# A state-space convolution and a gated linear unit on one core: three Fourier stages on sums and differences, split tokens kept in DRAM, and a new end of the program

## The chip, the core and the metric

The kernel runs on one of the eight cores of a Trainium2 chip. A core has a matrix engine (PE, with PEld for its weight loads), a vector engine (DVE), a scalar engine (ACT), GpSimd (POOL, used here to issue accumulating transfers), SyncE (SP, which issues the other transfers) and 16 DMA engines. Every engine works through its own instructions in order and waits on semaphores. The metric is device microseconds of one execution. Before the change three runs took 617.34, 618.17 and 620.17 us; the median is 618.17 us.

## The reference, cut to what matters

```
g = sigmoid((x * gate_w).sum(-1, keepdims=True))        # x is A_u, 2048 tokens x 512 channels
dt = exp(log_dt);  A = -exp(log_A_real) + 1j * A_imag;  C = (C_real + 1j * C_imag) * dt[:, None]
K = 2.0 * einsum("dn,dnl->dl", C, exp(A * dt * l)).real  # 512 channels, 128 states, l = 0..2047
a = irfft(rfft(x.T, 4096) * rfft(K, 4096))[:, :2048].T + x * D_skip
b = ((x @ w_gate) * (x @ w_up)) @ w_down                 # 512 -> 1792 -> 512, no nonlinearity
return g * a + (1 - g) * b
```

All of it is fp32. A convolution over 2048 tokens is done by Fourier transforms of length 4096, and a bilinear gated linear unit (GLU) over the same tokens is mixed with it.

## The kernel before, in words

**GLU.** The 1792 hidden features are 14 tiles of 128, taken in five groups (`GROUPS`: 3, 2, 3, 3, 3 tiles); inside a group the tokens pass in four sets of 512. Each fp32 operand is split into a high and a low fp32r part (`split`: a cast on ACT, a subtraction on DVE), and a product is three matmuls (low x high, high x low, high x high). `hidden(f)` makes 24 matmuls `pg` and `pu` of 128x512 for one tile of features, then ACT copies `pg` to `h`, DVE multiplies by `pu`, and ACT and DVE split the product into `hh` and `hl`. `down` multiplies by `w_down` into `y`: 12 matmuls per feature tile and set, so 36 per tile and set and 2016 in all. `evacuate` scales `y` by 1-g on ACT and sends it to the output, from the second group on as an accumulating transfer of POOL. `tokens` loads the four 128-channel pieces of a set and splits them, sixteen sets in all: four in the first group, three in each later one, since the order of the sets turns round from group to group.

**Convolution.** Channels go in 16 blocks of 32 for the kernel K and in 4 blocks of 128 for the transforms. For a block of 32, DVE and ACT make two tables of complex powers, `x` and `v` (`x_table`, `v_table`), and `k_block` multiplies them on PE (64 small matmuls, "kgen" below) into 2048 values of K, copied by ACT into `kt`. After each fourth block `k_first` takes the first Fourier stage of K. `u_part` does the same for the tokens, two columns of 128 rows at a time (eight parts), and DVE computes the gate's scores in it. Both stages write their spectra to DRAM (`su_d`, `sk_d`). `transforms(q)` then works on a block of 128 channels: `m_load` reads a quarter of both spectra, `m_second` is the second stage on PE, `m_product` the complex product on DVE, `m_inverse` the first inverse stage (through DRAM, `y_d`), `m_last` the last stage; its result is scaled by the gate and added to the output by POOL. "Second", "inverse" and "last" below are the PE tasks of these functions.

**Order.** Nothing is left to a scheduler: `Work` holds every piece as a task with an engine, a cost, a rank, what it reads and writes and the buffers that it holds. `Work.run` plans them on these costs and writes down each engine's order; `InOrder` binds the engines to it. `T_STEP` sets the earliest planned time of each GLU step. Every tile name has a fixed number of buffers, and a task that needs one waits for the last reader of the buffer's earlier content. A transfer that waits on SP holds up all that stand behind it on SP. The last rows of the output (set 3 of the last group) are finished in `ends`: they are read back into SBUF, added up there, and stored.

Of the kernel before, what the change touches and what calls it, by code (L numbers as in the profile page):

```python
# [10 lines left out]
F32 = mybir.dt.float32  # L11
# [3 lines left out]
ALU = mybir.AluOpType  # L15
# [27 lines left out]
N2 = list(range(1, 32, 2)) + list(range(2, 32, 4)) + list(range(0, 32, 8)) + list(range(4, 32, 8))  # L43
K_COLS = [[(0, 16, 16)], [(32, 8, 40), (48, 4, 52), (56, 4, 60)]]

def fourier_matrices():

    n1, k1 = np.arange(64), np.arange(64)
    ang = 2 * np.pi * np.outer(n1, k1) / 128
    c = np.stack([np.cos(ang), -np.sin(ang)], 2)
    c[:, 0, 1] = (-1.0) ** n1
    c = c.reshape(64, P)
    w1 = np.tile(c, (2, 1))
    w1k = np.tile(np.stack([c[2 * np.array(K_ROWS) + b] for b in range(2)], 1), (4, 1, 1))
    n2, k2 = np.array(N2), np.arange(32)
    w2 = np.zeros((2, 2, 32, 32, 2, 32))  # L60
    w3 = np.zeros((4, 32, 8, 2, 2, 2, 32))
    w4 = np.zeros((P, 64))
    s = 1 / 4096
    for k in range(64):
        S, j, e = k // 8, k // 2 % 4, k % 2
        q = k // 2
        if k:
            ph = 2 * np.pi * np.outer(n2, k + 128 * k2) / 4096
            co, si = np.cos(ph), np.sin(ph)
            w2[e, 0, :, q, 0], w2[e, 1, :, q, 0] = co, si  # L70
            w2[e, 0, :, q, 1], w2[e, 1, :, q, 1] = -si, co
            w3[j, :, S, e, 0, 0], w3[j, :, S, e, 0, 1] = 2 * s * co.T, 2 * s * si.T
            w3[j, :, S, e, 1, 0], w3[j, :, S, e, 1, 1] = -2 * s * si.T, 2 * s * co.T
            w4[2 * k], w4[2 * k + 1] = np.cos(ang[:, k]), -np.sin(ang[:, k])
            continue

        for l in range(1, 32):
            h, f = (0, 128 * l) if l < 16 else (1, 64 + 128 * (l - 16))
            ph = 2 * np.pi * n2 * f / 4096
            co, si = np.cos(ph), np.sin(ph)  # L80
            w2[0, h, :, 0, 0, l], w2[0, h, :, 0, 1, l] = co, -si
            w3[0, l, 0, 0, 0, h], w3[0, l, 0, 0, 1, h] = 2 * s * co, -2 * s * si
        w2[0, 0, :, 0, 0, 0], w2[0, 0, :, 0, 1, 0] = 1.0, (-1.0) ** n2
        w3[0, 0, 0, 0, 0, 0], w3[0, 0, 0, 0, 1, 0] = s, s * (-1.0) ** n2
        w4[0], w4[1] = 1.0, (-1.0) ** n1

    w4 = w4.reshape(2, 4, 2, 2, 4, 64).transpose(0, 2, 1, 3, 4, 5).reshape(P, 64)
    parts = (w1, w1k, w2.reshape(P, 32, 64), w3.reshape(P, 8, 2, 2, 64), w4)
    return [np.ascontiguousarray(a, np.float32) for a in parts]
# [24 lines left out]
T_STEP = 10.3  # L114
# [169 lines left out]
def gated_mix_kernel(  # L284
# [32 lines left out]
    m_su, m_sk, m_y, m_out = (work.memory() for _ in range(4))  # L317
# [12 lines left out]
    def inp(shape):  # L330
        return new("mid", "in", shape, bufs=3)
# [4 lines left out]
    half_pi = const.tile([P, 1], F32, name="half_pi")  # L336
    shift = const.tile([P, 1], F32, name="shift")
    gate = const.tile([P, NR], F32, name="gate")
    ngate = const.tile([P, NR], F32, name="ngate")
    score = const.tile([P, NR], F32, name="score")  # L340
# [4 lines left out]
    w1_t = tpool.tile([P, P], F32, name="w1_t")  # L345
    w1k_t = tpool.tile([P, 2, P], F32, name="w1k_t")
    skip = tpool.tile([P, 4, 32], F32, name="skip")
    m_const, m_powers, m_w1, m_w1k, m_skip = (work.memory() for _ in range(5))
# [3 lines left out]
    gw = new("mid", "bd", [P, D])  # L352
# [22 lines left out]
    def split(hi, lo, s, key):  # L375
# [5 lines left out]
        ph, pl = (hi, s), (lo, s)  # L381
        at = lambda x: x.t if s is None else x.t[:, s * D : (s + 1) * D]
        add("act", 0.62, lambda: act.copy(at(hi), src()), r=[got], w=[ph], rank=0)
        add(
            "dve", 0.69,
            lambda: dve.tensor_tensor(out=at(lo), in0=src(), in1=at(hi).bitcast(F32), op=ALU.subtract),
# [14 lines left out]
    def first_loads():  # L401
        in_y = lambda shape: new("mid", "y", shape, bufs=2)
        in_ev = lambda shape: new("mid", "ev", shape, bufs=3)
# [10 lines left out]
        for f in (1, 2):  # L414
            load_two(lambda k, f=f: ("w", f, k), in_ev, wts[f][:, : 2 * D].rearrange("p (k d) -> p k d", k=2))
# [51 lines left out]
    def product(pg, which, w, x, kt, after, first):  # L467
# [5 lines left out]
        def fn():  # L473
            for n, (a, b) in enumerate(three):
                pe.matmul(
                    pg.t, w[a].t[:, base : base + P], x[b].t, start=kt == 0 and n == 0, stop=kt == KT - 1 and n == 2
                )

        add("pe", 0.681, fn, r=[(w[0], part), (w[1], part), x[0], x[1]], w=[pg], rank=2, after=after)
# [43 lines left out]
    def evacuate(gi, ci, r, y):  # L523
        t = 4 * ci + r
        if gi == len(GROUPS) - 1 and ci == LAST:
            ending.append((r, y))
            return
        acc = new("glu", "acc", [P, D], bufs=3)
# [4 lines left out]

        if gi == 0:
# [7 lines left out]
    def ends():  # L542
# [7 lines left out]
        for r, y in ending:  # L550
            t = t0 + r
            add(
                "dve", 0.25,
                lambda r=r: dve.tensor_tensor(
                    out=sums.t[:, r, P * (KT - 1) :], in0=sums.t[:, r, P * (KT - 1) :], in1=late["fin"].t[:, r],
                    op=ALU.add,
                ),
                r=[late["fin"]], w=[(sums, r)], rank=0,
            )
            add(  # L560
                "dve", 0.69,
                lambda r=r, t=t, y=y: dve.scalar_tensor_tensor(
                    sums.t[:, r], y.t, ngate[:, t : t + 1], sums.t[:, r], op0=ALU.mult, op1=ALU.add
                ),
                r=[y, (m_gate, LAST)], w=[(sums, r)], rank=0,
            )
            add(
                "sp", 0.42, lambda r=r, t=t: sp.dma_start(ov[:, t, :], sums.t[:, r]), r=[(sums, r)], w=[(m_out, t)],
# [37 lines left out]
    def u_part(c):  # L606
        ut = inp([P, 2, D])
        add("sp", 0.42, lambda: sp.dma_start(ut.t, uv[:, 2 * c : 2 * c + 2, :]), w=[ut], dma=512, after=9.0 + 15.0 * c)

        def score_of(j):  # L610
            r = 2 * c + j
# [4 lines left out]
                    pr.t, ut.t[:, j, :], 1.0, gw.t, op0=ALU.mult, op1=ALU.mult, accum_out=score[:, r : r + 1]  # L616
                ),
                r=[ut, gw], w=[pr, (m_gate, ("s", c // 2))], rank=0,
            )


        banks = [[bank() for _ in range(2)] for _ in range(2)]
        sts = [stage([P, 2, D]) for _ in range(2)]

        def fn():
            for j in range(2):
                for h in range(2):
                    half = slice(64 * h, 64 * h + 64)
                    pe.matmul(
                        banks[j][h].t, w1_t[half], ut.t[half, j, :], start=True, stop=True, tile_position=(64 * h, 0)  # L630
                    )

        for j in range(2):
            score_of(j)
        add("pe", 2.08, fn, r=[ut, m_w1], w=banks[0] + banks[1], rank=1, hold=sts)
# [687 lines left out]
```

## Time and profile before

| | |
|---|---|
| median of three runs | 618.17 us |
| profiled execution, first to last instruction | 615.6 us |
| around the span, against the median | 2.6 us |
| PE / DVE / ACT / POOL busy | 605.5 / 514.9 / 420.1 / 88.6 us |
| moved by DMA | 121.67 MB, 198 GB/s in the mean |
| last matmul starts, end of the span | 610.70 us, 615.6 us |

The profile gives no time of its own for the profiled execution besides the span; it lies 2.6 us under the median of the runs. A row of the groups names engine, operation, output<-inputs by tile names and shape, and then busy time and mean duration. All rows carry line 100, the helper that records an instruction (line 120 after the change), so work is told apart by tile names. Matmuls follow each other faster than they last: a duration of 390 ns stands beside a step of about 227 ns from one start to the next. fp32 matmuls are recorded twice, so a task of 64 of them shows as x128. `in`, `ts`, `ev`, `kt`, `x`, `v` are SBUF tiles, `k` the PSUM banks of the convolution.

### The profile page before, as it was taken

What the parts mean: (1) busy time and instruction counts of PE and PEld (TensorE: products, weight loads), DVE (VectorE), ACT (ScalarE), POOL (GpSimd) and SP (SyncE); (2) the same over time, 40 slices, a digit from 0 to 9 for tenths busy, and PEclk for the clock granted to TensorE, in tenths of its full rate; (3) what the DMA queues carried; (4) which work ended last, traced back from release to release, by engine and by line L of the source; (5) the groups of instructions that cost most, each with busy time, mean ns of one, the idle gap of its engine ahead of it and who ended that gap; (6) DMA issues with size and microseconds to landing.
All of it is one profiled execution on the core that took longest, in us unless ns stands there. A gap on an engine that the chain in (4) does not pass through costs nothing.

```text
span 615.6 us, 17970 instructions
## 1 busy us (share of the span) xinstructions
PE 605.5 (98%) x7524; PEld 468.9 (76%) x7524; DVE 514.9 (84%) x810; ACT 420.1 (68%) x953; POOL 88.6 (14%) x125
## 2 busy tenths in 40 slices
PE   8999999999999999999999999999999999999996
PEld 5776777788777788887768888786888887678865
DVE  6958999999999999999889999999999842377342
ACT  5469877896878886679688768878885663533320
POOL 0211111111112201010120202021110101210120
PEclk9999999999999999999999999999999999999999
DMA  8795736555677977748797939787996789897771
GB/s 284 221 283 181 242 111 199 171 180 119 158 198 189 234 206 191 172 121 206 245 229 181 235 112 229 221 239 167 196 237 194 188 232 308 205 278 199 170 107 69
DMA packets 103238, 121.67 MB, mean 198 GB/s; under 512 B 6644, under 2 KB 66548, under 8 KB 102900
## 3 DMA queue, kind: packets, MB, share of 16 engines
q1 hardware_dynamic: 83732, 92.33, 49.3%
q0 software_dynamic: 19008, 28.06, 25.4%
q8 instruction: 59, 0.97, 0.6%
q14 instruction: 23, 0.19, 0.1%
q10 hardware_dynamic: 416, 0.13, 0.1%
HBM read 69.37 MB, written 51.12 MB: 196 GB/s over the span
## 4 chain that ended last, share of the span: by engine, by line
PE 75%; issue 10%; DMA 7%; DVE 4%; ACT 3%; POOL 1%; POOLq 0%; ACTq 0%; DVEq 0%
PE pg L100 20%; PE y L100 19%; PE pu L100 19%; PE k L100 18%; DMA out<-acc 3%; DMA raw<-in_xT 3%; ACT acc L100 1%; ACT ts L100 1%; DMA y<-in_xT 1%; DVE xlo L100 1%; POOL out L100 1%; ACT rt L100 1%; POOL su_d L100 1%; DVE v L100 1%; DVE t L100 1%
## 5 line engine op out<-in xcount | busy, mean ns | idle before, releaser
L100 POOL DMA_DIRECT2D out<-acc x60 | 51.3, 891 | 369.1 <-ACT acc L100 327.2
L100 PE MATMUL y<-dhi,hl 128*128 128x512 f32 x224 | 90.7, 405 | 1.5 <-ACT acc L100 0.9
L100 PE MATMUL pg<-xhi,wlo 128*128 128x512 f32 x224 | 90.3, 403 | 0.4 <-ACT h L100 0.3
L100 PE MATMUL pg<-xlo,whi 128*128 128x512 f32 x224 | 87.8, 392 | 1.6 <-issue 1.2
L100 PE MATMUL pu<-xhi,wlo 128*128 128x512 f32 x224 | 89.3, 399 | 0.0
L100 PE MATMUL pg<-xhi,whi 128*128 128x512 f32 x224 | 87.7, 392 | 0.5 <-ACT whi L100 0.5
L100 PE MATMUL y<-dhi,hh 128*128 128x512 f32 x224 | 87.5, 390 | 0.0
L100 PE MATMUL y<-dlo,hh 128*128 128x512 f32 x224 | 87.4, 390 | 0.0
L100 PE MATMUL pu<-xhi,whi 128*128 128x512 f32 x224 | 87.4, 390 | 0.0
L100 PE MATMUL pu<-xlo,whi 128*128 128x512 f32 x224 | 87.4, 390 | 0.0
L100 ACT ACTIVATE acc<-y,ngate 128x512 f32<-128x512 f32 x76 | 51.8, 692 | 29.9 <-PE y L100 18.4
L100 DVE TENSOR_TENSOR h<-pu,h 128x512 f32<-128x512 f32 x56 | 38.5, 688 | 39.7 <-PE pu L100 39.4
L100 ACT CAST hh<-h 128x512 fp32r<-128x512 f32 x56 | 34.9, 623 | 38.3 <-DVE h L100 38.2
L100 ACT COPY ts<-k 128x512 f32<-128x512 f32 (+1 forms) x112 | 47.7, 503 | 13.8 <-PE k L100 13.7
L100 PEld LDWEIGHTS y<-dhi,hl 128*128 128x128 f32 x224 | 42.0, 188 | 18.6 <-issue 2.7
L100 PEld LDWEIGHTS pg<-xhi,wlo 128*128 128x128 f32 x224 | 42.1, 188 | 18.1 <-issue 7.8
L100 ACT COPY h<-pg 128x512 f32<-128x512 f32 x56 | 32.9, 588 | 30.7 <-PE pg L100 24.5
L100 PEld LDWEIGHTS pu<-xhi,wlo 128*128 128x128 f32 x224 | 42.0, 188 | 12.7 <-issue 3.0
L100 PEld LDWEIGHTS pg<-xhi,whi 128*128 128x128 f32 x224 | 42.1, 188 | 12.5 <-ACT whi L100 2.1
L100 PEld LDWEIGHTS y<-dhi,hh 128*128 128x128 f32 x224 | 42.0, 188 | 9.3
L100 PEld LDWEIGHTS pu<-xhi,whi 128*128 128x128 f32 x224 | 42.2, 188 | 9.0
L100 PEld LDWEIGHTS pg<-xlo,whi 128*128 128x128 f32 x224 | 42.2, 188 | 8.8 <-DVE xlo L100 0.7
(109 smaller groups left out, 1169.5 us busy)
## 6 DMA issues: line engine op xcount, KB each, us to landing
raw<-in_xT SPq DMA_DIRECT2D x60, 256.0 KB, 4.6
out<-acc POOLq DMA_DIRECT2D x60, 256.0 KB, 6.7
raw<-in_wts SPq DMA_DIRECT2D x36, 256.0 KB, 4.4
su_d<-ts POOLq DMA_DIRECT2D x32, 256.0 KB, 4.6
y_d<-ts SPq DMA_DIRECT2D x16, 512.0 KB, 4.7
sk_d<-ts SPq DMA_DIRECT2D x14, 512.0 KB, 5.3
in<-sk_d SPq DMA_DIRECT2D x12, 512.0 KB, 6.8
in<-su_d SPq DMA_DIRECT2D x12, 512.0 KB, 5.4
```

The lines of the kernel that those rows point to most:

```text
L100: got = getattr(self.engine, name)(*args, **kw)
```

## The change

- **Sums and differences.** With a token's number written as 32 n1 + n2, the four tokens of n1 or 63-n1 and n2 or 31-n2 now share a partition (`place`). `u_part` takes four columns of tokens at once (four parts instead of eight); DVE makes their sums and differences (two operations of 1024 elements, four of 512), so that the first stage contracts over 32 rows instead of 64. `k_block` does it for K: ACT copies one half out of PSUM reversed, DVE adds and subtracts (two operations of 256 elements per block of 32) into `kt`. `m_second` then needs real factors alone: 32 matmuls of 32x32 tiles over 256 columns instead of 64 matmuls of 64x32 over 128. `m_last` makes even and odd parts (eight matmuls of 64x32 per half of the tokens), and ACT and DVE put them together by a copy, a sum and a difference. `v`'s powers stand at strides of 2 and 4 elements instead of side by side, and `kt` is written in steps of 32 elements.
- **Split tokens in DRAM.** The first group's split tokens are written to `xs_d` (16 writes of 512 KB); the later groups read both parts from there (48 reads of 512 KB) instead of loading and splitting again.
- **Rank.** DVE operations of the third channel block's spectra get rank 2 (`late_rank`), behind the fourth block's tables.
- **Tiles.** The last block's spectra, stages and results use the table tiles (`x`, `v`, `ri`, `e`, `t`, `rt`); the results of the third and the fourth block for the last set's rows are added in SBUF (before, of the fourth alone). `in` and `ev` have two buffers of twice the size.
- **Last GLU rows.** The last set's `y` is evacuated by ACT into SBUF (`acc`, `raw`) and added there, instead of being held in PSUM.
- `T_STEP` is 9.85 instead of 10.3, and `after` of `u_part` steps by 20.

```diff
-T_STEP = 10.3
+T_STEP = 9.85
+U_STEP = 20.0
...
     def inp(shape):
-        return new("mid", "in", shape, bufs=3)
+        return new("mid", "in", shape, bufs=2)
...
     def tokens(gi, ci, kt):
-        x = xs[kt] = [new("glu", n, [P, D], F32R, 5) for n in ("xhi", "xlo")]
+        x = xs[kt] = new("glu", "xs", [P, 2, D], F32R, 5)
+        if gi:
+            add("sp", 0.42, lambda: sp.dma_start(x.t.bitcast(F32), xs_d[ci, kt]), r=[(m_xs, (ci, kt))], w=[x], dma=512, rank=0)
+            return
         load(("x", gi, ci, kt), xT[kt * P : (kt + 1) * P, ci * D : (ci + 1) * D])
-        split(x[0], x[1], None, ("x", gi, ci, kt))
+        split(x, x, (0, 1), ("x", gi, ci, kt))
+        add("sp", 0.42, lambda: sp.dma_start(xs_d[ci, kt], x.t.bitcast(F32)), r=[x], w=[(m_xs, (ci, kt))], dma=512, rank=2)
...
+        ones = [new("mid", "y", [P, 2, D], bufs=2) for _ in range(2)]
+        ops = (ALU.add, ALU.subtract)
+        for y, op in zip(ones, ops):
+            add(
+                "dve", 1.22,
+                lambda y=y, op=op: dve.tensor_tensor(out=y.t, in0=ut.t[:, :2], in1=ut.t[:, 2:], op=op), r=[ut], w=[y],
+            )
+        for s, op in enumerate(ops):
+            for d, y in enumerate(ones):
+                add("dve", 0.69, ...
+        def first(s):
+            banks, st = [bank() for _ in range(4)], new("mid", "ev", [P, KT, 4, P], bufs=2)
+            def fn():
+                for p in range(2):
+                    col, src = 64 * (p + s), 2 * s + (p + s) % 2
+                    for tq in range(4):
+                        lanes = slice(32 * tq, 32 * tq + 32)
+                        pe.matmul(
+                            banks[tq].t[64 * p : 64 * p + 64], w1_t.t[lanes, col : col + 64], ut.t[lanes, src],
+                            start=True, stop=True, tile_position=(32 * tq, 64 * p),
+                        )
...
-        for to, of, n in ((32, 0, 16), (56, 32, 8)):
+        for to, of, n in (((33, 64, 2), (0, 16, 1), 16), ((34, 64, 4), (33, 49, 2), 8)):
...
+        side = lambda h: kt.t[:, h, :, :, g0 : g0 + 8].rearrange("p b k g -> p g b k")
+        add("act", 0.6, lambda: act.copy(side(1), pv(0)[:, :, :, ::-1]), r=[pk], w=[(kt, (1, b % 4))])
+        for h, op in enumerate((ALU.add, ALU.subtract)):
+            add(
+                "dve", 0.45, lambda h=h, op=op: dve.tensor_tensor(out=side(h), in0=pv(1), in1=side(1), op=op),
+                r=[pk, (kt, (1, b % 4))], w=[(kt, (h, b % 4))], rank=0,
+            )
...
+    def late_rank(q):
+        return 2 if q == KT - 2 else 1
...
     def m_second(q, ins, w):
+            for f in range(8):
+                c, h = f % 4, f // 4
+                for r in range(4):
+                    lanes = slice(32 * r, 32 * r + 32)
+                    pe.matmul(
+                        banks[r].t[32 * c : 32 * c + 32, 2 * P * h : 2 * P * h + 2 * P], w.t[lanes, f],
+                        src[lanes, f].rearrange("p w d -> p (w d)"), start=True, stop=True,
+                        tile_position=(32 * r, 32 * c),
+                    )
...
+    def m_last(q, gs):
+                for tq in range(4):
+                    for p in range(2):
+                        lanes = slice(64 * p, 64 * p + 64)
+                        pe.matmul(
+                            bs[p].t[32 * tq : 32 * tq + 32], w4_t[lanes],
+                            t.t[lanes, 4 * tq : 4 * tq + 4].rearrange("p n d -> p (n d)"), start=True, stop=True,
+                            tile_position=(64 * p, 32 * tq),
+                        )
...
+            add("act", us - 0.1, lambda cut=cut, odd=odd, side=side: act.copy(side(1), cut(odd)), r=[odd], w=[(fin, 1)])
+            for s1, op in enumerate((ALU.add, ALU.subtract)):
+                add("dve", us, ...
+        for q, gs in {KT - 2: [], KT - 1: [(q - 1, (0, 1)), (q, (0,)), (q, (1,))]}.get(q, [(q, (0, 1))]):
+            m_last(q, gs)
```

SP's order in the first 20 us, from the loads of the parameters on. Before (`raw` are weights and tokens as loaded, `in` the columns of `u_part`, `bd` and `w3s` hold the gate's weights):

```order
L100 DMA raw<-in_wts 128x512 x2
L100 DMA bd<-in_rows 128x512
L100 DMA w_t<-in_w 128x128
L100 DMA v<-in_prm 128x1024
L100 DMA in<-in_u 128x1024
L100 DMA dt_d<-small 128x4
L100 DMA raw<-in_wts 128x512
L100 DMA raw<-in_xT 128x512
```

The same place after the change:

```order
L120 DMA raw<-in_wts 128x512 x2
L120 DMA w3s<-in_rows 128x512
L120 DMA w2s<-in_w 128x192
L120 DMA v<-in_prm 128x1024
L120 DMA xs_d<-xs 128x1024 x4
L120 DMA in<-in_u 128x2048
L120 DMA dt_d<-small 128x4
L120 DMA raw<-in_wts 128x512
L120 DMA raw<-in_xT 128x512
```

Four writes of split tokens and a twice as large `in` now stand ahead of the third down weight (`raw<-in_wts` in the last row but one).

DVE's order between the third `h` and the fourth, in the second GLU set. Before, the end of that stretch:

```order
L100 SCALAR_TENSOR_TENSOR y,score<-in,bd 128x512
L100 SCALAR_TENSOR_TENSOR x<-x 128x512
L100 SCALAR_TENSOR_TENSOR y,score<-in,bd 128x512
L100 SCALAR_TENSOR_TENSOR v<-x 128x16x32
L100 SCALAR_TENSOR_TENSOR v<-v,x 128x16x32
L100 TENSOR_TENSOR t<-v,turns 128x672
L100 TENSOR_SCALAR gate<-score 128x4
L100 TENSOR_SCALAR ngate<-score 128x4
L100 TENSOR_TENSOR xlo<-raw,xhi 128x512 x2
L100 TENSOR_TENSOR h<-pu,h 128x512
```

After the change, the middle of that stretch:

```order
L120 TENSOR_TENSOR xs<-raw,xs 128x512
L120 SCALAR_TENSOR_TENSOR y,gate<-in,w3s 128x512
L120 SCALAR_TENSOR_TENSOR v<-x 128x16x32
L120 SCALAR_TENSOR_TENSOR v<-v,x 128x16x32 x2
L120 TENSOR_SCALAR ngate<-gate 128x4
L120 TENSOR_SCALAR gate<-gate 128x4
L120 SCALAR_TENSOR_TENSOR v<-v,x 128x16x32
L120 TENSOR_TENSOR y<-in 128x1024 x2
L120 TENSOR_TENSOR t<-v,turns 128x672
L120 TENSOR_TENSOR in<-y 128x512
L120 TENSOR_TENSOR xs<-raw,xs 128x512 x2
L120 TENSOR_TENSOR in<-y 128x512 x3
```

The sums and differences (`y<-in`, `in<-y`) stand here, and PE's first `u_part` task needs the second `in<-y`; before it needed only the load.

PE's order at the last `m_last`. Before (`k<-v,w_t` is that task):

```order
L100 MATMUL pg<-xhi,wlo 128x512
L100 MATMUL pg<-xlo,whi 128x512
L100 MATMUL pg<-xhi,whi 128x512
L100 MATMUL k<-v,w_t 64x512 x8
L100 MATMUL pg<-xhi,wlo 128x512
L100 MATMUL pg<-xlo,whi 128x512
L100 MATMUL pg<-xhi,whi 128x512
L100 MATMUL pu<-xhi,wlo 128x512
```

After the change, at the very end of PE's order:

```order
L120 MATMUL y<-dhi,hl 128x512
L120 MATMUL y<-dlo,hh 128x512
L120 MATMUL y<-dhi,hh 128x512
L120 MATMUL k<-x,w_t 32x512 x16
L1395 UNCONDITIONAL_BRANCH
```

Before, 75 GLU matmuls follow the last `m_last`; after the change none does.

More of the change, by code (lines that the diff above doesn't have):

```diff
@@ L524, in evacuate @@
         t = 4 * ci + r
[L525 to L528, printed above, removed]
+        final = gi == len(GROUPS) - 1 and ci == LAST
+        acc = new("glu", "raw", [P, D], bufs=2) if final and r == 3 else new("glu", "acc", [P, D], bufs=3)
         add(
@@ L1079, in m_product @@
+        add("pe", 1.15, fn, r=[*parts, w], w=banks, rank=1, hold=[to], many=apart_of(q))
+        for r in range(4):
+            p, e = divmod(r, 2)
+            evict(
+                q, r, 0.59, lambda p=p, e=e: to.t[:, :, e, p].rearrange("p w (h d) -> p w h d", h=2),
+                lambda r=r: banks[r].t.rearrange("p (h w d) -> p w h d", h=2, w=2), [banks[r]], [(to, r)],
+            )
+        return to
+    def m_product(q, T, uk):
         shape = [P, 2, 2, 2 * P]
         y = new("mid", "y", shape, bufs=2)
-        z = new("mid", "bd", shape)
@@ L1108, in m_inverse @@
     def m_inverse(q, T0, ys, ws):
-        banks, sts = [bank() for _ in range(4)], [stage([P, 2, 2, 2, P]) for _ in range(2)]
+        banks, shape = [bank() for _ in range(4)], [P, 2, 2, 2, P]
+        if q == KT - 1 and T0:
+            sts = [new("tab", n, shape) for n in ("ri", "e")]
+        else:
+            sts = [stage(shape) for _ in range(2)]
         def fn():
```

509 lines of the change are left out of this document (262 added, 247 removed).

## The prediction

> **What bounds the kernel now.** I read the page first (busy shares, slices, chain), then busy time by stretch, then groups and single tasks. The page's rows: busy time of each engine, DVE and DMA in 40 slices of 15.4 us (tenths), and the chain that ended last.
>
> ```profile
> span 615.6 us, 17970 instructions
> ...
> PE 605.5 (98%) x7524; PEld 468.9 (76%) x7524; DVE 514.9 (84%) x810; ACT 420.1 (68%) x953; POOL 88.6 (14%) x125
> ...
> DVE  6958999999999999999889999999999842377342
> ...
> DMA  8795736555677977748797939787996789897771
> ...
> PE 75%; issue 10%; DMA 7%; DVE 4%; ACT 3%; POOL 1%; POOLq 0%; ACTq 0%; DVEq 0%
> ```
>
> PE is busy for 98% of the span and carries 75% of the chain. But DVE's nines reach from slice 5 to slice 31, and DMA has nines of its own. By stretch (us and length; then busy us of PE, PEld, DVE, ACT, POOL with counts, clock, DMA share, GB/s):
>
> ```profile
> 0.00:20.00 20.00, 18.05 (x62) 12.64 (x63) 14.84 (x42) 10.71 (x19) 0.96 (x25) 1.00 0.79 261
> ...
> 60.00:100.00 40.00, 40.00 (x291) 29.56 (x291) 39.89 (x66) 32.08 (x65) 8.93 (x12) 1.00 0.60 187
> ...
> 250.00:300.00 50.00, 50.00 (x678) 39.85 (x664) 48.94 (x74) 38.25 (x87) 3.42 (x4) 1.00 0.70 190
> ...
> 500.00:520.00 20.00, 20.00 (x253) 15.29 (x252) 6.22 (x14) 8.31 (x17) 3.10 (x4) 1.00 0.99 262
> 520.00:540.00 20.00, 20.00 (x208) 14.26 (x207) 7.93 (x12) 9.59 (x25) 3.42 (x3) 1.00 0.94 241
> 540.00:560.00 20.00, 19.85 (x442) 15.85 (x441) 13.23 (x22) 8.20 (x14) 3.46 (x4) 1.00 1.12 292
> ```
>
> PE never stops, the granted clock is 1.00, DVE has 2 to 3% left while the tables are made, and from 500 us on DMA is full. Work taken from PE is therefore worth its full price only as far as DVE and DMA follow.
>
> **The change on PE.** Single tasks of the timeline (start, length, count of records), and two GLU matmuls ten steps apart:
>
> ```profile
> 20.65 1.99 PE L100 MATMUL k<-in,w_t 64*128 64x512 f32 x8
> 166.12 2.00 PE L100 MATMUL k<-kt,w1k_t 32*128 32x512 f32 x16
> 232.10 2.06 PE L100 MATMUL k<-in,w2s 64*32 64x128 f32 x128
> 309.82 2.79 PE L100 MATMUL k<-in,w_t 128*64 128x512 f32 x12
> 312.44 1.03 PE L100 MATMUL k<-y,w_t 128*64 128x512 f32 x4
> 501.11 2.07 PE L100 MATMUL k<-v,x 128*32 128x64 f32 x128
> 584.78 0.39 PE L100 MATMUL pu<-xlo,whi 128*128 128x512 f32 x1
> 587.05 0.39 PE L100 MATMUL pu<-xhi,whi 128*128 128x512 f32 x1
> ```
>
> A GLU matmul takes (587.05-584.78)/10 = 0.227 us; 2016 of them, 458 us, stay. With 0.35 us for each of the 61 changes between GLU and convolution (what the GLU's stretches take beyond the 458 us, an estimate that holds their small waits too), and the other tasks at their rows, PE's order sums to 609; the trace has the last matmul end at 611.1. So PE's order with prices from rows gives the time before, and I use the same sum for the change.
>
> - `u_part`: eight tasks of 1.99 us become eight of eight matmuls that fill the array once, like the two of the row of 1.03 us; at 1.0 that is 7.7 us less.
> - `m_second`: sixteen of 2.06 us. Half the matmuls at twice the columns, on sixteen tiles instead of eight. No row shows sixteen tiles at a time. Low end: array full, 1.03, 16 us less. High end: eight at a time as now, 2.06, nothing less. I take 1.03, since every task above takes 2.0 us for two fillings of the array, whether in two, four or eight tiles.
> - `m_last`: 2.6 + 1.0 us for each of four blocks becomes 1.9; 6.7 us less. `k_first` stays at 1.95. Kgen and inverse stay.
> - Four more changes between kinds of work: 1.4 us more.
>
> Not charged: ACT, which loses 25 us of splits and 8 of `kt` and gains about 8 of copies at 68% busy; POOL's 32 writes of `su_d`, the same bytes in as many issues; the 1 MB reads of `y_d` in place of two of 512 KB each, which lie tens of us ahead of their use in PE's order; the lower rank of the third block's products, which is in the DVE sums below. What covers the last two is DMA's idle time, and it is nearly gone from 500 us on.
>
> Sum on PE: 7.7 + 16.2 + 6.7 + 0.2 - 1.4 = 29.4 us less.
>
> **DVE.** Prices by group (count, then busy us, mean ns); one instruction follows the last about 80 ns before its end.
>
> ```profile
> L100 DVE TENSOR_TENSOR xlo<-raw,xhi 128x512 fp32r<-128x512 f32 x60 | 40.2, 686 | 10.1 <-ACT xhi L100 9.9
> ...
> L100 DVE TENSOR_TENSOR y<-ev 128x1024 f32<-128x1024 f32 x16 | 19.5, 1221 | 3.8 <-ACT ev L100 3.3
> ...
> L100 DVE TENSOR_TENSOR v<-v,sq 128x256 f32<-128x256 f32 x16 | 6.7, 421 | 0.1
> ```
>
> So 0.60, 1.14 and 0.34 us for 512, 1024 and 256 elements. Gone: 48 splits, 29 us (ACT loses 25). New: `u_part` 8x1.14 + 16x0.60 = 18.7; `kt` 32x0.34 = 10.8; `m_last` and the end about 10. Net +11 us. More telling is where: priced so in its order, DVE has 60.6 us of work up to the first kgen before and 86.7 now; up to the last kgen 453.5 before and 457.3 now. PE's own order reaches these at 77 and 499 before, at 88 and 476 now. At the first kgen DVE has no slack left; from there to the last PE has 388 us of work and DVE 371 (379 with the 2% by which these prices, 504 us in all, fall short of DVE's 514.9). DVE just keeps up, if it does not wait for others more than 2% of the time. Where DVE is late, PE waits at the kgen and with it all GLU matmuls behind it, since PE takes nothing out of turn. I charge 2 us for that and for the transfers of the last block's spectra (bounds: 0, and the 9 us of its slack lost and as much again on PE).
>
> **The start.** Here the new DVE and DMA work has no cover.
>
> ```profile
> 9.98 0.65 SPq L100 DMA_DIRECT2D in<-in_u  x1
> 16.62 0.33 SPq L100 DMA_DIRECT2D raw<-in_wts  x1
> 21.89 0.69 DVE L100 TENSOR_TENSOR dlo<-raw,dhi 128x512 fp32r<-128x512 f32 x1
> 26.38 0.68 DVE L100 TENSOR_TENSOR h<-pu,h 128x512 f32<-128x512 f32 x1
> 42.45 0.69 DVE L100 TENSOR_TENSOR h<-pu,h 128x512 f32<-128x512 f32 x1 [3.65 <-PE pu L100]
> ```
>
> DMA moves 261 GB/s in the first 20 us. Four writes and half a load, 2.6 MB, now go ahead of the third down weight: 10 us at that rate, of which some 5 lie beside the idle stretch that the queue had after 16 us. So `dlo`, at 21.9 before, comes near 28, while PE, without the first `u_part`, wants it near 26: about 3 us. Then PE reaches the first `u_part` 30 GLU matmuls later, near 36; on DVE 15 us of instructions stand between the third `h` (at 24 by PE) and the second `in<-y`, which gives 39: 3 us more, and 1 us at the next set. Start: 7 us, bounds 0 (DMA and DVE both have room) and 10 (all of the 2.6 MB shows).
>
> **The reloads.** A piece of split tokens can be fetched only once its buffer is free, that is when the last `pu` of the old set has read it. By PE's order 21 matmuls lie between that and its use at the first reload, 4.8 us; at the other sets 6.1, 6.4, twice 9.1, 8.2, and 13.6 or more at six. SP waits in its order meanwhile, so the other pieces, and weights that stand between them, go later too; PE waits for the pieces, and DVE and ACT for PE's next `pg` and `pu`.
>
> ```profile
> in<-in_u SPq DMA_DIRECT2D x8, 512.0 KB, 5.8
> ...
> v<-sk_d SPq DMA_DIRECT2D x4, 512.0 KB, 9.7
> ...
> out<-kt SPq DMA_DIRECT2D x4, 256.0 KB, 2.0
> ...
> out<-ts POOLq DMA_DIRECT2D x1, 256.0 KB, 7.5
> ```
>
> At 5.8 us the first is late by 1 and the pieces behind it by as much again: 3 us. At 9.7, as in the full stretch, six sets are late by 5.2, 3.9, 3.6, 0.9, 0.9 and 1.8: 16 us. Bounds 0 and 16; I take 3, since the three short covers lie between 125 and 170 us, where DMA is half to three quarters busy.
>
> **The end.** The last task of PE is now `m_last`, and what follows it is no longer hidden.
>
> ```profile
> 592.72 2.87 POOL L100 DMA_DIRECT2D out<-ts  x2 [4.62 <-DVE ts L100]
> ...
> 606.68 5.56 SPq L100 DMA_DIRECT2D out<-kt  x4
> ...
> 610.70 0.39 PE L100 MATMUL y<-dhi,hh 128*128 128x512 f32 x1
> 611.13 0.75 DVE L100 SCALAR_TENSOR_TENSOR kt<-y,ngate,kt 128x512 f32<-128x512 f32 x1 [1.29 <-PE y L100]
> ```
>
> Before: 611.1 to 615.6, 4.5 us (one DVE operation, a store of 2.0, the closing 1.7). Now: the first half of `m_last` ends 1 us before PE does; a copy on ACT 0.6, on DVE 1.2 + 0.34 + 1.14, then POOL issues 512 KB (1.6 of the pair's 2.87 us) and 256 KB, which lands 7.5 us after its issue: 11.6 us after PE, and with the closing 13.3. That is 8.8 more (bounds 5 and 10).
>
> **Sum.** 615.6 - 29.4 + 8.8 + 7 + 3 + 2 = 607.0 us of span. The profiled execution lies 2.6 under the median of 618.17, so 609.6, written 610. With three of the four losses at half or at half again: 603 to 616.
>
> **Rivals.**
>
> *The losses at the start and at the reloads don't come* (DMA orders itself better, DVE fills its early gaps, 16 us of idle time in the first 60). Then 615.6 - 29.4 + 8.8 + 2.6 = 598. For it: DVE's many waits at the start. Against it: the first kgen's 86.7 us of DVE work.
>
> *DVE becomes the bound, by strided writes.* 32 operations on `kt` and 32 on the powers of stride four now write element by element in steps of 4 to 32 elements. ACT's rows show what that can cost: its `kt` copy, which already wrote so, takes 1127 ns, a plain copy of as many elements 595. DVE's rows say otherwise as far as they go: clears of 1, 128 contiguous and 32 strided elements take 0.06, 0.17 and 0.09 us, 1 ns an element each way.
>
> ```profile
> L100 ACT COPY ts<-k 128x512 f32<-128x512 f32 x60 | 31.8, 595 | 8.2 <-PE k L100 8.2
> ...
> L100 ACT COPY kt<-k 128x512 f32<-128x512 f32 x16 | 18.0, 1127 | 15.4 <-PE k L100 15.3
> ```
> ```profile
> 1.36 0.06 DVE L100 MEMSET shift<- 128x1 f32 x1
> 1.39 0.17 DVE L100 MEMSET skip<- 128x128 f32 x1
> ...
> 55.72 0.09 DVE L100 MEMSET v<- 128x32 f32 x1
> ```
>
> At ACT's surcharge of 1.04 ns an element, 64 x 0.27 = 17 us more DVE work, 9 of them in its slack: 618, or 627 if that slack is used up by waits. It decides once DVE's work between the first and last kgen passes PE's 388 us, so from 9 us on. The Trainium skill, SBUF — State Buffer, "Door 1: The DMA port swizzle", says that SBUF has lines of 16 bytes and that each access to a new line pays; by that rule DVE would pay as ACT does, and the sum would be this rival's; ACT's row agrees with it, DVE's clears do not.
>
> *The reloads land late everywhere*, at 9.7 us: 13 us more than charged, 623. For it: DMA at 0.94 to 1.12 from 500 us on, and some 20 MB more to move. *Sixteen tiles don't run at once*: `m_second` keeps 2.06 us, 626.
>
> **Chances.** Forecast 0.46, full gain 0.20, strided writes 0.13, late reloads 0.10, no sixteen tiles 0.06, others 0.05. The bound of half a per cent (615.1 and 621.3), about what a measurement of this kernel can tell from none, cuts them thus: faster 0.41 of the forecast, all of the full gain and 0.01 of the rest, 0.62; within it 0.05 of the forecast, 0.07 of the strided case and 0.02 of the rest, 0.14; slower 0.24. The range goes from 597 to 628: from the full gain to the late cases' ends.
>
> **What the next profile would show.** Right: `m_second` in about 1.0 us; PE waiting for DVE near 26 to 45 us; `xs` named as releaser at the first reloads; 13 us from the last matmul to the end. Wrong: `kt<-k,kt` on DVE well over 421 ns; `m_second` at 2 us; PE idle for `xs` at most of twelve sets; or PE with almost no idle time before 60 us, which would make it the full gain.

## The result: a quarter slower

The changed kernel takes 767.29 us (median of 4 runs, 763.61 to 772.13), the kernel before 617.75 us beside it: 1.2405 times as long, 95% interval 1.2341 to 1.2469. The forecast was 610 with a range from 597 to 628. Times are medians of fast runs; a fourth run of e1, at 688.26 us, counts as slow and is left out. PE has fewer instructions than before (6500 matmul records, 7524 before), is busy for as long (605.8 us, 605.5 before, at a granted clock of 0.90 in the mean and not 1.00) and stands still for a fifth of the span. From the page of the changed kernel: the span, busy shares, the 40 slices (19.2 us each) of PE, DVE, the granted clock and DMA, and the chain that ended last.

```profile
span 767.7 us, 15856 instructions
...
PE 605.8 (79%) x6500; PEld 453.9 (59%) x6500; DVE 537.4 (70%) x841; ACT 403.8 (53%) x919; POOL 86.9 (11%) x125
...
PE   8897998899984999930979999907699993991292
...
DVE  7996895999964999990269999907699541670034
...
PEclk9998999999996999985889999967899996996596
DMA  9999985677747875543479858227896859653295
...
PE 39%; DMA 33%; DVE 18%; ACT 5%; issue 3%; SPq 0%; POOL 0%; DVEq 0%; ACTq 0%
```

Before, PE carried 75% of the chain and DMA 7%; now DMA carries a third. In the two slices where PE has a 0, DVE has a 0 too, and DMA a 3 and a 2: no engine works and the DMA engines are mostly idle, so it is not too many bytes. The waits name transfers (engine and line, what was waited for: us in total, times, longest):

```profile
PE pg L120 <- DMA xs<-xs_d: 38.7, 2, 31.9
...
ACT ts L120 <- DMA sk_d<-ts: 34.5, 3, 28.9
PE k L120 <- DMA in<-y_d: 31.2, 2, 17.8
...
PE k L120 <- ACT ts L120: 24.8, 2, 24.2
...
PE k L120 <- DMA in<-sk_d: 15.3, 2, 10.3
```

The longest stop, at 334 us, shows how they hang together. First SP's queue there (start, us, count of DMAs), then stretches of the same place (start, end and length; busy us of PE, PEld, DVE, ACT, POOL; clock, DMA share, GB/s):

```profile
317.52 1.12 SPq L120 DMA_DIRECT2D in<-y_d  x2
324.89 22.23 SPq L120 DMA_DIRECT2D xs<-xs_d  x4
347.21 30.95 SPq L120 DMA_DIRECT2D sk_d<-ts  x4
```
```profile
320.00:334.00 14.00, 13.82 (x68) 10.06 (x66) 13.97 (x18) 9.27 (x21) 0.00 (x0) 1.00 0.12 51
...
340.00:344.00 4.00, 0.00 (x0) 0.00 (x0) 3.97 (x5) 0.00 (x0) 0.00 (x0) 0.50 0.93 280
364.00:376.00 12.00, 10.07 (x43) 6.96 (x44) 0.00 (x0) 2.52 (x7) 0.86 (x1) 0.76 0.13 54
```

From 320 to 334 us only the two 1 MB reads of `y_d` are under way, and the 16 DMA engines are busy to 0.12, which is two of sixteen; they move 51 GB/s, so that 1 MB takes 20 us and both take 41. The four loads of `xs` behind them are held twice. SP takes 22 us to issue them, where four issues take about 2 (the two reads took 1.12): the trace has no packet of theirs before 337 us. Then most engines are through with them by 350 (0.93 at 340 us), but on two engines their pieces come after what is left of the reads, which lasts to 364 us. PE needs whole tiles, and stands still from 334 to 366 us. The `sk_d` writes behind fare alike: from 364 us two engines are still at their last pieces. Counted over the span from the trace's packets (512 bytes and more), exactly two are in flight for some 95 us and exactly four for some 59, before for some 9 and 6.

The trace also has the times at which each transfer's semaphore was raised, and they show the engines one by one. An `xs` load raises it sixteen times; of the first load behind the reads fourteen of these fall between 342.0 and 344.0 us, and the last two at 364.9 and 365.9 us, just when PE goes on. A read of `y_d` raises it once about 1 us after its issue starts and then only twice: at 340.0 and 341.4 us for the first of the two, at 363.7 and 364.7 for the second. The `sk_d` writes do so once and then four times. The reads of `y_d` in the kernel before raise it sixteen times.

What lets a transfer use two engines stands in the diff. The DRAM side of the read is `"(k p) n d -> p k (n d)", p=2`: its outermost dimension is 2. That of the writes of `su_d` and `sk_d`, `"(t a) n d -> a t (n d)", a=4`, is 4. The patterns of these three tensors in the kernel before begin with 128 (32 in the last block), and the changed kernel's own reads of the last block are issued by halves `p` and begin with 32. On POOL's queue the issue to landing of the `su_d` writes, 256 KB each, tells the same, the changed kernel first:

```profile
su_d<-ev POOLq DMA_DIRECT2D x32, 256.0 KB, 14.8
```
```profile
su_d<-ts POOLq DMA_DIRECT2D x32, 256.0 KB, 4.6
```

This is theory A in the experiments: few engines, and whatever is queued behind on them waits. Rival B there is that the added bytes, the reloads and the two buffers stall the kernel. The Trainium skill, DMA: Bandwidth & Descriptors, section "Why a DMA increments its semaphore by 16 and not by 1", states the number of engines as a rule: a transfer is spread over the largest number up to 16 that divides the outermost dimensions (above 1) of both patterns. By it the reads get 2 engines and the writes 4; the 0.12 above agrees for the reads, and so do the two and four raised semaphores for the reads and the `sk_d` writes.

### The profile page after: what moved, and what is told of

The parts are those of the page before. It is cut to its first block, busy times and chain, and to the rows that moved or that the text cites. A ratio compares the mean times of both kernels' runs of the same rounds, so it can differ in the third digit from the quotient of the medians.

```text
span 767.7 us, 15856 instructions
## 1 busy us (share of the span) xinstructions
PE 605.8 (79%) x6500; PEld 453.9 (59%) x6500; DVE 537.4 (70%) x841; ACT 403.8 (53%) x919; POOL 86.9 (11%) x125
## 4 chain that ended last, share of the span: by engine, by line
PE 39%; DMA 33%; DVE 18%; ACT 5%; issue 3%; SPq 0%; POOL 0%; DVEq 0%; ACTq 0%
PE pg L120 11%; PE y L120 10%; PE pu L120 10%; DMA sk_d<-ts 10%; DMA xs<-xs_d 8%; PE k L120 8%; DMA in<-y_d 6%; DVE v L120 4%; DMA su_d<-ev 3%; DVE x L120 3%; DMA in<-in_u 2%; DVE y L120 2%; DVE h L120 1%; DVE hl L120 1%; DVE kt L120 1%
## 5 line engine op out<-in xcount | busy, mean ns | idle before, releaser
L120 PE MATMUL pg<-xs,whi 128*128 128x512 f32 x448 | 140.7, 395 | 4.5 <-issue 3.1
L120 PE MATMUL pu<-xs,whi 128*128 128x512 f32 x448 | 140.2, 395 | 0.0
L120 PE MATMUL pg<-xs,wlo 128*128 128x512 f32 x224 | 91.3, 408 | 40.3 <-DMA xs<-xs_d 38.7
L120 PEld LDWEIGHTS pg<-xs,whi 128*128 128x128 f32 x448 | 85.6, 191 | 24.2 <-issue 3.6
L120 PEld LDWEIGHTS pu<-xs,whi 128*128 128x128 f32 x448 | 85.5, 191 | 17.2
L120 PE MATMUL pu<-xs,wlo 128*128 128x512 f32 x224 | 91.5, 408 | 3.1 <-DVE h L120 3.1
L120 PEld LDWEIGHTS pg<-xs,wlo 128*128 128x128 f32 x224 | 42.7, 191 | 58.8 <-DMA xs<-xs_d 39.8
L120 ACT COPY ev<-k 128x512 f32<-128x512 f32 x88 | 46.9, 593 | 38.4 <-PE k L120 30.1
L120 PEld LDWEIGHTS pu<-xs,wlo 128*128 128x128 f32 x224 | 42.7, 191 | 25.5 <-issue 11.6
L120 PEld LDWEIGHTS y<-dlo,hh 128*128 128x128 f32 x224 | 43.3, 193 | 9.9 <-DVE dlo L120 1.9
## 6 DMA issues: line engine op xcount, KB each, us to landing
su_d<-ev POOLq DMA_DIRECT2D x32, 256.0 KB, 14.8
```

The source lines that it names most:

```text
L120: got = getattr(self.engine, name)(*args, **kw)
```

## The experiments

e1 to e3 and e7 start from the changed kernel, e4 to e6 from e3, e9 and e10 from e4, e11 and e12 from e9, and e8 from the kernel before. All but e6, e10 and e12 keep the order of instructions on PE, DVE and ACT of the kernel that they start from; in those three the planner orders anew.

**e1, wide reads.**

```
-sp.dma_start(t.t, rows_y)          # rows_y: p k (n d), p=2
+for p in range(2):
+    sp.dma_start(t.t[64 * p : 64 * p + 64], rows_y[p])
```

> Only the six 1 MB reads of y_d are changed: each is issued as two reads of 64 rows, so that the outermost dimension of the DRAM pattern is 64 and not 2; order of tasks, bytes, buffers are the same. Theory A (a transfer runs on only so many of the 16 DMA engines as the outermost dimension of its pattern lets it: 2 for y_d, 4 for sk_d and su_d; what is queued behind on these engines waits): the 8 KB packets, which now run 2 at a time at about 50 GB/s and take 20 us per MB, run 16 at a time; the 32 us wait of pg for xs goes, as do most of the waits for y_d; 640 to 690 us. Rival B (the reloads of split tokens, the added bytes and the two buffers of in and ev make the stalls, whatever the pattern): 750 to 770 us, no change beyond a per cent or two.

679.94 us, ratio to the kernel before 1.1027 (1.0939 to 1.1115): 87 us gone with six reads split in two. Exactly two packets are in flight for some 9 us, and PE's waits for `xs` are down to this:

```profile
PE pg L120 <- DMA xs<-xs_d: 6.6, 1, 6.6
```

**e2, wide writes.**

```
-pool_q.dma_start(su_d[...], st.t[:, q])     # a t (n d), a=4; the same for sk_d on SP
+for a in range(4):
+    pool_q.dma_start(rows_u[a], st.t[32 * a : 32 * a + 32, q])
```

> Only the writes of su_d and sk_d are changed: each is issued as four writes of 32 rows in place of one with an outermost dimension of 4; 144 more issues, 96 of them on POOL. Theory A: the first 150 us lose their small waits for ev and su_d, the kgen wait for ts near 220 us (24 us) goes; the y_d reads still block; 715 to 750 us. Rival B: 760 to 775 us, a little slower by the issues.

713.2 us, ratio 1.1533 (1.1494 to 1.1571), 54 us less than the changed kernel and a little better than the lower end. Four packets are in flight for some 6 us, two still for some 102. Two stretches, e2 first, then the changed kernel:

```profile
200.00:250.00 50.00, 49.46 (x692) 37.90 (x690) 48.98 (x73) 36.56 (x89) 6.09 (x7) 1.00 0.93 243
300.00:350.00 50.00, 16.57 (x73) 11.98 (x72) 17.14 (x25) 13.89 (x33) 3.48 (x4) 0.66 0.43 111
```
```profile
200.00:250.00 50.00, 35.71 (x331) 26.08 (x324) 33.42 (x47) 27.70 (x58) 6.96 (x8) 0.87 0.61 158
300.00:350.00 50.00, 33.88 (x392) 26.50 (x391) 46.21 (x66) 30.61 (x71) 5.24 (x6) 0.89 0.56 140
```

The first stretch, with the first `sk_d` writes, is full now; the second, with the first `y_d` reads, is not.

**e3, both edits.**

> Both edits. Theory A: nearly all of the long waits go; what remains of the loss against the forecast is the strided writes on DVE (64 operations at 0.63 to 0.68 us in place of 0.42: 15 us of DVE work), m_second at 1.4 us in place of 1.0, and the reloads: 610 to 645 us. Rival B: 745 to 770 us.

625.22 us, ratio 1.0114 (1.008 to 1.0148). The two edits give 142 us together, 87 and 54 apart: a sum. Rival B is out: the bytes, the reloads and the two buffers are all still there, and no wait for `xs` is among PE's longest any more. The longest is now this one:

```profile
PE pg L120 <- ACT h L120: 5.9, 2, 5.8
```

**e4, the same writes in a quarter of the issues.**

```
-for q in range(KT): for a in range(4):      # 16 of 64 KB for each of the eight tasks
-    pool_q.dma_start(su_d[q, rows a, n0 : n0 + 4], st.t[lanes a, q])
+for a in range(4):                          # 4 of 256 KB, "f (t a) n d -> a t f (n d)"
+    pool_q.dma_start(su_d[:, rows a, n0 : n0 + 4], st.t[lanes a])
```

> As e3, but each set of su_d rows leaves in four writes of 32 rows by four blocks (256 KB each) in place of sixteen of 64 KB: 32 issues on POOL's queue and not 128, the order on PE, DVE and ACT unchanged. Theory A (what is left at the start is ACT waiting 8 us for ev, held by POOL's queue of small writes, and PE waiting 6 us for h behind it): POOL busy falls from 128 to about 85 us, the wait near 80 us goes; 5 to 10 us less than e3, 615 to 620 us. Rival C (what is left is DVE and PE, both full from 100 to 500 us): within 2 us of e3, 623 to 627 us.

616.41 us, ratio 0.9958 (0.9925 to 0.9991); the loads of `su_d` wait here for all of its writes. From 60 to 100 us, e3 and then e4:

```profile
60.00:100.00 40.00, 34.19 (x171) 24.78 (x170) 30.84 (x53) 24.12 (x55) 27.19 (x56) 0.91 0.80 253
```
```profile
60.00:100.00 40.00, 38.30 (x208) 26.98 (x206) 37.70 (x64) 31.15 (x68) 8.71 (x16) 1.00 0.90 297
```

POOL gives 8.7 us to issues and not 27, ACT no longer waits for `ev`, PE gains 4 us, and the first kgen comes at 100.1 us and not at 106.0.

**e5, `kt` written in a row, read by PE in steps.**

```
-kts["now"] = new("tab", "kt", [P, 2, 2, 16, 32])      # h b k g
+kts["now"] = new("tab", "kt", [P, 2, 32, 2, 16])      # h g b k
```

> As e3, but the sums and differences of kt are written without strides (256 elements in a row), and the reading on PE's side steps by 128 bytes instead. Theory D (DVE pays for each strided element; these 32 operations fall from 677 to about 420 ns): 8 us less DVE work; if DVE bounds the stretch from 100 to 500 us, 617 to 620 us; if PE does, 623 to 626 us. Either way the mean of kt<-k,kt says whether the stride is the cause. Rival E (the cause is PSUM as a source of both size and order, not the stride of the write): the mean stays near 677 ns.

635.57 us, ratio 1.025 (1.0217 to 1.0283). The groups of e3 and of e5 (count, then busy us, mean ns), and one task of k_first in e5:

```profile
L120 DVE TENSOR_TENSOR kt<-k,kt 128x256 f32<-128x256 f32 x32 | 21.7, 677 | 2.5 <-ACT kt L120 2.4
```
```profile
L120 DVE TENSOR_TENSOR kt<-k,kt 128x256 f32<-128x256 f32 x32 | 13.4, 417 | 2.5 <-ACT kt L120 2.3
```
```profile
187.20 3.70 PE L120 MATMUL k<-kt,w1k_t 32*128 32x512 f32 x16
```

Theory D is right on the price: the steps in `kt`, which the operation reads and writes, are what costs DVE. But PE, reading every 32nd element, takes 3.6 us for a task that took 1.9: eight of them are 13.6 us, and the kernel is 10 us slower, outside both of D's times. DVE's 8 us made up for little of it. This points at PE as the bound of the middle, but two things changed at once; e9 separates them.

**e6, tokens split again.**

```
-if gi:
-    add("sp", 0.42, lambda: sp.dma_start(x.t.bitcast(F32), xs_d[ci, kt]), ...)
-    return
 load(("x", gi, ci, kt), ...)
 split(x, x, (0, 1), ("x", gi, ci, kt))
-add("sp", 0.42, lambda: sp.dma_start(xs_d[ci, kt], x.t.bitcast(F32)), ...)
```

> As e3, but the tokens are loaded and split for each set again as in the kernel before (no xs_d): 48 splits more on ACT and DVE, 16 writes of 512 KB and 24 KB per partition of reloads less on the queue. Theory F (the split tokens in DRAM pay, since DVE is full): DVE work rises by 29 us, time rises by 10 to 25 us, to 635 to 650 us. Rival G (the reloads and the early writes cost as much as the splits): within 5 us of e3.

672.18 us, ratio 1.0828 (1.0782 to 1.0873): 47 us more than e3, twice the upper end of theory F, at 564.4 us of DVE work for 535.7. F has the sign. The size it doesn't explain: 29 us of splits don't make 47, and the planner's order is another one here. Rival G's time, within 5 us of e3, didn't come, but with another order the run doesn't separate what the splits cost from what the order costs (10 and 17 us in e12 and e10).

**e7, the narrow reads on another queue.**

```
-"sp", 0.42, lambda t=t, g=g: sp.dma_start(t.t, y_d[q] ...)
+"pool", 0.95, lambda t=t, g=g: pool_q.dma_start(t.t, y_d[q] ...)
```

> The changed kernel as it is, with its six two-engine reads of y_d issued from POOL and not from SP; pattern, bytes and buffers stay. Theory A1 (the long stalls come mostly from what stands behind these reads in SP's queue on the same two engines): the 32 us wait of pg for xs goes, xs reloads land in 5 to 10 us, only waits for y_d itself stay; 690 to 720 us. Theory A2 (they come from the slow read itself, wherever it is queued, m_last being late): 750 to 770 us.

727.26 us, one run: 40 us less than the changed kernel, between A1 and A2. Its wait of PE for `xs`:

```profile
PE pg L120 <- DMA xs<-xs_d: 16.5, 6, 4.2
```

The 32 us wait is gone (the longest for `xs` is 4.2 us). By this one run, standing in SP's queue ahead of other transfers accounts for some half of the 87 us that the reads cost; the rest stays when they stand in POOL's. PE's waits for the reads themselves fall from 31.2 us to 5.5. How the rest is shared between a late `m_last`, the engines used by other transfers too, and what now waits behind the reads in POOL's queue, these runs don't tell.

**e8, the narrow read alone, in the kernel before.**

```
-rows_y = y_d[q].rearrange("k (h r) d -> k h r d", h=2)[:, :, r : r + 4]
+rows_y = y_d[q].rearrange("(k p) (h r) d -> h p k (r d)", p=2, h=2)[..., P * r : P * r + 4 * P]
+for h in range(2): sp.dma_start(t.t[:, 0, h], rows_y[h])     # rows of w4 in the same order
```

> The kernel before, with its reads of y_d (twelve of 512 KB in the first three blocks) issued as 24 of 256 KB whose DRAM pattern has an outermost dimension of 2 (rows in the order even, odd, with the rows of w4 in the same order) in place of 128; nothing else of the change. Theory A: these reads run on two engines at 40 GB/s, 13 us for each 512 KB and 157 us in all, and hold up what stands behind them in SP's queue: 670 to 720 us. Rival B (few engines matter only in the changed kernel, because of its two buffers and reloads): 617 to 630 us.

726.93 us, ratio 1.175 (1.1695 to 1.1806), 7 us above theory A's range. One shape of one read (24 reads of 256 KB for twelve of 512) costs the kernel before 108 us, with its three buffers, without reloads, with its own order. A stretch of it:

```profile
303.00:320.00 17.00, 0.06 (x1) 0.00 (x0) 0.00 (x0) 0.00 (x0) 0.00 (x0) 0.65 0.13 50
```

All five engines stand still for 17 us while two of the sixteen DMA engines (a share of 0.13) move 50 GB/s, where the expectation had 40. Rival B falls here too.

**e9, `kt` in runs of 16.**

```
-kts["now"] = new("tab", "kt", [P, 2, 2, 16, 32])      # h b k g
+kts["now"] = new("tab", "kt", [P, 2, 2, 32, 16])      # h b g k; the copies to ts read PSUM in steps of 16
```

> As e4, but kt lies in runs of 16 elements as DVE and ACT write them, PE reads it in a row, and the copies of its PSUM banks to ts read PSUM in steps of 16 elements. Theory D (DVE pays for each new 16-byte line it writes, PE for each it reads): kt<-k,kt falls from 672 to about 420 ns, k_first stays at 1.93 us (in e5 it took 3.63), and since PE and not DVE bounds the middle the time is 0 to 4 us under e4. Rival H (the copies that read PSUM in steps now cost as much more): ts<-k over 0.6 us for 256 elements and a time at or above e4.

616.26 us, ratio 0.995 (0.9927 to 0.9973): no different from e4.

```profile
L120 DVE TENSOR_TENSOR kt<-k,kt 128x256 f32<-128x256 f32 x32 | 13.4, 420 | 2.4 <-ACT kt L120 2.3
...
L120 ACT COPY ts<-k 128x256 f32<-128x256 f32 x52 | 15.7, 391 | 1.5 <-PE k L120 1.5
```

Runs of 64 bytes are as cheap as one row, the copies that read PSUM in steps cost no more than before (395 ns in e4), so rival H is out; and 6 us less of DVE work leave the time as it was. The stretch between the kgens tells why, e4 first, then e9:

```profile
100.00:490.00 390.00, 387.61 (x4659) 299.75 (x4659) 383.62 (x566) 292.05 (x680) 52.39 (x60) 1.00 0.84 212
```
```profile
100.00:490.00 390.00, 389.14 (x4681) 301.99 (x4671) 380.92 (x571) 293.37 (x684) 53.45 (x62) 1.00 0.85 214
```

In e4 PE is idle for 2.4 of these 390 us, so PE bounds the middle and there was little for DVE to give back; from the first to the last kgen e9's profile has 390 us and e4's 393, and e9's first kgen comes 2 us later.

**e10, the writes of split tokens later.**

```
-sp.dma_start(xs_d[ci, kt], ...), ..., dma=512, rank=2)
+sp.dma_start(xs_d[ci, kt], ...), ..., dma=512, rank=2, after=30.0)
```

> As e4, but the writes of split tokens to xs_d are put behind 30 us in the planner's time, so that none stands ahead of the third down weight; the planner then orders the rest of the start anew. Theory J (these writes cost the start some 3 to 5 us, the waits near 26 us): 611 to 614 us. Rival K (the start is bound by DVE's work before the first kgen, which stays): within 2 us of e4, 615 to 619 us.

633.55 us, ratio 1.0222 (1.0175 to 1.0269), 17 us more than e4: neither theory's number. The planner's order of the start changed with it, and PE now waits 9.1 us for the splits on ACT. With the order changed, what the early writes cost by themselves stays open.

**e11, `m_second` in diagonals; e12, truer durations for the planner.**

```
-for f in range(8): c, h = f % 4, f // 4
-    for r in range(4): ...
+for n in range(32): h, r = n // 16, n % 4; c = (r + n // 4) % 4; f = 4 * h + c ...
```

> As e9, but the 32 matmuls of m_second go out in diagonals: each next one lies in another row and another column of tiles, where they now fill one column of tiles after the other. m_second takes 1.42 us, its first sixteen matmuls start 6.6 ns apart and the second sixteen 0.65 us later and 16 ns apart. Theory L (the order of the tiles makes the second set wait): the task falls to about 1.05 us, 16 times, and the time by up to 6 us, 610 to 613 us. Rival M (the second set of weights can't be loaded beside the first set's matmuls, whatever the order): 1.42 us stays and 614 to 618 us.

```
-add("pe", 1.15, fn, ...)       # m_second; powers of v: 0.04 * n + 0.08
+add("pe", 1.45, fn, ...)       # powers of v: 0.70 and 0.63
```

> As e9, with the planner's durations of m_second and of the powers of v set to what the trace shows (1.45 us; 0.70 and 0.63 us on DVE, 1.2 and 1.05 on ACT); the planner then orders all engines anew. Theory N (true durations give an order with fewer waits): 608 to 614 us. Rival O (the order is as good as it gets by chance, and another one loses as e10 did): 618 to 635 us.

e11: 615.99 us, ratio 0.9951 (0.9923 to 0.9979), `m_second` still 1.43 us, so theory L is out; that the second weights are what waits (M) is not shown by it. e12: 626.67 us, ratio 1.0136 (1.0098 to 1.0174), as rival O has it. The two other orders of the planner cost 10 us (e12 against e9) and 17 (e10 against e4), and truer single prices don't make the order better.

## Why the prediction was wrong

**The step that failed** is the one that cost two edits at nothing: "Not charged: ... POOL's 32 writes of `su_d`, the same bytes in as many issues; the 1 MB reads of `y_d` in place of two of 512 KB each, which lie tens of us ahead of their use". It counted bytes and issues and took a transfer's duration from rows of other shapes (5.8 us for 512 KB, 7.5 for a store). The shape had changed: outermost dimension 2 and 4 in place of 128. In their place the runs show 87 us for the reads (e1), 54 for the writes of `su_d` and `sk_d` (e2), 142 for both (e3). The writes of `sk_d` were in no sum at all. None of the rivals had this mechanism: "reloads late everywhere" named the right wait, `xs`, with the wrong cause and a tenth of the price. The words "lie tens of us ahead of their use" held for the first two blocks, whose `m_last` didn't wait for its reads; for the third PE was there 16 us after the issue of its two reads (675.6 and 692 us), these took 49 us, and PE waited for them for 31.2 us. What the words missed besides is what stands behind such a read on the same engines.

With the shapes mended (e4, a span of 614.6 us) the sum of 607.0 us can be held against the trace term by term:

| term | forecast | e4 |
| --- | --- | --- |
| `m_second`, each of 16 | 1.03 us | 1.42 us, +6.2 in all |
| `u_part`; `m_last` in pairs; `k_first` | 1.0; 1.9; 1.95 | 1.04; 1.88; 1.93 |
| start | first kgen near 95 (88 and 7) | 100.1, against 80.0 before |
| first to last kgen on PE | 388 us | 393.0 us, 4.3 of it `m_second` (11 of its 16 tasks) |
| reloads | 3 us | no wait of PE, 5.7 us to landing |
| last matmul to the end | 13.3 us | 14.5 us |

The first and the last kgen, one task of `m_second` between them and the last task of e4 (start, length; a task's length to the start of the next work is some 0.07 us less, 1.42 for `m_second`), then two groups on DVE and the reloads' time to landing:

```profile
100.10 2.07 PE L120 MATMUL k<-v,x 128*32 128x64 f32 x128
...
220.96 1.49 PE L120 MATMUL k<-in,w2s 32*32 32x256 f32 x64
...
493.07 2.07 PE L120 MATMUL k<-v,x 128*32 128x64 f32 x128
...
595.75 4.36 PE L120 MATMUL k<-x,w_t 64*32 64x512 f32 x32 [1.53 <-issue]
```
```profile
L120 DVE TENSOR_TENSOR kt<-k,kt 128x256 f32<-128x256 f32 x32 | 21.5, 672 | 2.4 <-ACT kt L120 2.4
...
L120 DVE TENSOR_TENSOR v<-v,sq 128x256 f32<-128x256 f32 x16 | 10.1, 633 | 1.2 <-ACT sq L120 1.2
...
xs<-xs_d SPq DMA_DIRECT2D x48, 512.0 KB, 5.7
```

- *PE's sum.* Right in its parts but for `m_second`. Sixteen tiles do run at once: the first sixteen matmuls start within 0.1 us of each other. The second sixteen come 0.65 us after the first, where 0.52 would fill the array, and start further apart. The rival "sixteen tiles don't run at once", 2.06 us, is out; what holds the second set is open, e11 showing only that it is not the order of the tiles.
- *DVE.* The strided rival had the price right and the forecast had it wrong: `kt<-k,kt` takes 672 ns for 421, and the powers of stride four 633 for 421, so DVE has 535.6 us of work, 21 more than before and not 11. But it did not decide, as the rival said it would from 9 us on: with some 15 us of surcharge DVE is busy for 383.6 of the 390 us from 100 to 490 and PE for 387.6, so DVE still just kept up, and e9 takes 6 us of it away and the time stays. The clears from which I argued against it misled.
- *The Trainium skill's 16-byte lines.* The Trainium skill, SBUF — State Buffer, "Door 1: The DMA port swizzle", was weighed against DVE's clears and set aside. The trace agrees with the page: steps of 16 bytes and more cost half as much again, while the powers of stride two, 8 bytes, stay at 690 to 696 ns for 512 elements (685 before).
- *Start, reloads, end.* The first kgen comes 5 us later than the 88 by PE's order and the 7 charged; the reloads lost nothing and the 2 us for DVE and the last spectra don't show as a wait; the end was right to 1.2 us. The errors left, 6.2 + 5 + 1.2 - 3 - 2, come to 7.4, and e4's span is 7.6 over the sum. That the two nearly agree is in part luck, since losses and charges that didn't come cancel.
- *Slips in the working.* Sixteen times 1.03 us are 16.5, not the 16.2 of the sum, whose 0.2 has no line of its own. At 9.7 us the six late sets come to 14.5 us; the recorded delays go with 10.0. Neither matters beside 142.
- *The check list.* `m_second` at 1.0 us didn't come; PE waited for DVE near 26 us, but for 1 to 2 us only (`dlo`); `xs` as releaser came, but at 334 us and not at the first reloads, and for another reason than thought; about 13 us at the end came (14.9 in the changed kernel, 14.5 in e4). The list had no line for a DMA share of 0.12 with PE idle, which is where the answer stood.

So the change, done with wide transfers and with the `su_d` writes merged, is worth 0.4 to 0.5% (e4, e9, e11; the intervals reach from 0.1 to 0.8%), not the 1.4% of the forecast. These three versions, the best that were run, are not told apart: e9 has 616.26 us against 619.08 for the kernel before beside it, e11 615.99 against 619.26.

## What to carry to other kernels

Before costing a moved transfer by its bytes, write down the outermost dimension of both of its patterns; with 2 in place of 128 a read of 1 MB took 20 us and more, with 4 a write of 256 KB landed after 14.8 us and not 4.6, and this cost 54 to 108 us here at the same bytes. Splitting it into 2 or 4 transfers whose rows come first takes the loss back, and the issues saved by merging them otherwise (e4 against e3) count as well. Where PE is idle and the DMA share is near 2/16 (0.12 and 0.13 here), look for such a transfer at the head of the queue and not for the one that the wait names.

## What the runs showed of the hardware that was not expected

- A narrow transfer holds up wide ones behind it in the same queue, and even their issue: `xs<-xs_d` lands 5.7 us after its issue in e4; behind two narrow reads four such issues took 22 us and PE waited 31.9 us.
- A long stop costs PE more than its length: the granted clock is 0.50 in the stop and 0.76 in the 12 us from 364 us. In e3, after a stop of 6 us from 80.8 us on, GLU matmuls come 427 ns apart for some 4 us, where the median is 227.
- PE pays for steps in its moving operand: 1.93 us a task with elements in a row, 3.63 at steps of 128 bytes. Reading PSUM in steps of 64 bytes cost ACT nothing (391 ns against 395).
